# Linear attention beside a gated linear unit on one core: the query features transposed in 32x32 blocks by VectorE and stored feature-major, in place of 128x128 transposes by TensorE in the output stage

## The chip, the cores and the metric

The kernel runs on one core of one Trainium2 chip. The metric is the device time of one execution in microseconds (us). The profiler's engine names are used: PE is TensorE, DVE is VectorE, ACT is ScalarE, POOL is GpSimd, SP is SyncE, which here issues the DMA transfers. All data is float32; matmul operands are written as a rounded high part and a rest (type fp32r), so that three matmuls make one product.

## The reference, cut to what matters

```python
xn = layernorm(x)                                  # x: [2048, 1024]
qkv = xn @ wqkv                                    # 32 heads of 32
pq, pk = q @ w_phi, k @ w_phi                      # per head
phi_q = concat([softmax(pq), softmax(-pq)])        # 64 features a head
phi_k = concat([softmax(pk), softmax(-pk)])
kv, z = phi_k.T @ v, sum(phi_k)                    # per head
s = (phi_q @ kv) / (phi_q @ z + 1e-6) @ wo
h = sigmoid(xn @ w_gate) * (xn @ w_up)             # F = 3584
g = silu(h @ w_down)
out = x + s * g
```

The changed part is phi_q: 2048 tokens with 32 x 64 = 2048 features each. It is made with tokens on partitions, since softmax and the denominator reduce over features; the product phi_q @ kv contracts over features, so it wants features on partitions.

## The kernel before, in words

The large products are done by a seven-product scheme (B11, B21, T2, T3, T4, T1, B22 name its products), each product as three matmuls at lines 145 to 147 (`mm3`). The stages run one after another on TensorE: layer norm and projections, the GLU in passes (in the second of them the k features and kv sums of all heads are made beside it), then the down product and the output stage.

**The down product** has 112 steps: 84 of 24 matmuls, then 28 of 12. For each step SP loads a weight block (line 916) and one or two blocks of h (line 918), ScalarE writes the high part of each (line 136) and VectorE the rest (line 137); both together are a split. `tick()` counts groups of 12 matmuls; `later(n, f)` asks for work n ticks on. In this stage 32 units of query features, 16 token tiles t by two halves hb of the heads, are finished, one every 24/5 ticks (`q_late`). A unit is a buffer `e` of 128 tokens by 1024 features. For t from 6 on it is made here: extremes (663, 664), differences (673, 674), exponentials (ScalarE, 677), sums and reciprocals (682, 683). The 12 units with t under 6 were made earlier, stored in `e_d`, and are loaded again. All are weighed with z on GpSimd (995), reduced to the denominator on VectorE (1000 to 1006), scaled on GpSimd (1013) and stored to `e_d` by one transfer of 512 KB (1016). A scheduler that simulates the engines at build time sets the order on each engine here, within what `behind()` ties to the matmuls.

**The output stage** runs over eight pairs of token tiles. In a pair, (hb, q) names a quarter of the features, 512 of them. `e_load` (1042) brings 128 tokens u by a quarter, `transposes` (1052) turns it with four TensorE transposes into a PSUM bank, and `phi_part` writes from that bank the high part (ScalarE, 1064) and the rest (VectorE, 1066), 512 columns each; the two tiles u of the pair lie side by side. `numerators` (1076) multiplies with kv (`nm` in the table below, four matmuls each), `numerators_out` copies one half of the bank (ScalarE, 1083, `cp`) and adds the other (VectorE, 1085, `ad`). `o_sum` (GpSimd, 1090) and `o_part` (1099, 1101) make the operands of the output product of the next pair; `products` (`g`, groups of three matmuls), `product_out` (`v`), `scaled` (GpSimd, 1957 and 1958, `m` and `a`) and `store` finish the current one. The first pair's features are turned by `attend()` beside the last 14 steps of the down product. For the other seven the written-out table `PAIR` fixes the order on all five engines: `tr`, `hi`, `lo`, `e` are the steps just named, with the digits of u, hb and q; a trailing + or - shifts a name to the next or the previous pair. The last pair's products follow a table `LAST`.

Of the kernel before, what the change touches and what calls it, by code (L numbers as in the profile page):

```python
# [18 lines left out]
P = 128  # L19
# [8 lines left out]
HB = 512  # L28
EPS_LN = 1e-5
# [20 lines left out]
def hedgehog_glu_kernel(  # L50
# [28 lines left out]
    e_d = dram.tile([TT, 2, P, 2 * HB], F32, name="e_d")  # L79
# [35 lines left out]
    QA = 6  # L115
# [550 lines left out]

    def spread(st, p, e):
# [124 lines left out]
    def z_broadcast(hb, i):  # L792
# [4 lines left out]
        nc.scalar.copy(zacc[:, i * HB:(i + 1) * HB], kvb[i])  # L797
        if i:
            nc.sync.dma_start(zb_d[hb], zacc)
# [141 lines left out]
    eqr = Ring((50, 51, 24, 25))  # L941
# [5 lines left out]
    def q_steps(at, t, hb):  # L947
# [16 lines left out]
        for n, f in ((0, load), (5, first), (6, lambda: spread(hold[2], *hold[:2])), (8, lambda: exponentials(hold[1])),  # L964
                     (9, sums), (10, keep)):
            later(at + n, f)

    def q_late(at, t, hb):
# [16 lines left out]
        def second():  # L985
            hold["e"] = whole(eqr.next())
            spread(hold["st"], hold["p"], hold["e"])
# [9 lines left out]
        def density():  # L997
# [4 lines left out]
            den = st[:, 4]  # L1002
            nc.vector.tensor_reduce(den, d2.rearrange("p (h t) -> p h t", t=2), axis=AX.X, op=ALU.add)
            nc.vector.tensor_scalar_add(den, den, EPS_DEN)
            nc.vector.reciprocal(den, den)
            nc.vector.tensor_mul(r2.rearrange("p (h t) -> p h t", t=2), r.rearrange("p (h t) -> p h t", t=2),
                                 den[:, :, None].to_broadcast([P, 16, 2]))
# [6 lines left out]

        def keep():
            nc.sync.dma_start(e_d[t, hb], hold["e"])
# [3 lines left out]
        for n, f in steps + ((11, weigh), (14, density), (15, scale), (18, keep)):  # L1020
            later(at + n, f)
# [10 lines left out]
    tpr, nmr, amm = Ring(banks[:2]), Ring(banks[2:4]), Ring(banks[4:])  # L1032
# [6 lines left out]
    def e_load(u, q):  # L1039
        tp_, hb = divmod(e_next[u, q], 2)  # L1040
        if tp_ < NTP:
            nc.sync.dma_start(slots[47 + u][:, q], e_d[2 * tp_ + u, hb, :, q * HB:(q + 1) * HB])
        e_next[u, q] += 1

    tbank, nbank, half = {}, {}, set()

    def transposes(u, hb, q):
        tbank[u, hb, q] = ps = tpr.next()
        e = whole(47 + u)
        for j in range(4):  # L1050
            k = 4 * q + j
            nc.tensor.transpose(ps[:, j * P:(j + 1) * P], e[:, k * P:(k + 1) * P], ident)  # L1052
        if (hb, q) in half:
            half.remove((hb, q))
        else:
            half.add((hb, q))
            b = run(phu.next(), 2).rearrange("p a b n -> p (a b n)")
            units_ph[hb, q] = b.rearrange("p (a k t) -> p a k t", a=2, t=256)

    def phi_part(part, u, hb, q):  # L1060
        ph, cs = units_ph[hb, q], slice(u * P, (u + 1) * P)
# [993 lines left out]
```

## Time and profile before

| what | value |
|---|---|
| median of three runs | 2331.45 us (2328.89 to 2331.76) |
| span of the profiled execution | 2328.9 us |
| the profiled execution's own time | 2328.89 us, the lowest of the three |
| granted TensorE clock | 0.999 |
| down product | 1577 to 2117 us of the span |
| first transposes of the output stage, last | 2075 us, 2294 us |
| query units stored | 1630 to 2035 us |

Times in the trace count from the span's start. A row of a group reads: line, engine, operation, output<-inputs, shapes, count, then busy us and mean ns of one, then the engine's idle time just before and what ended it. The matmuls are pipelined: one of 512 columns is shown as 0.39 us long, and the next starts 0.23 us after it, so distances between starts are read and not lengths. VectorE's rows overlap in the same way by 0.08 us.

### The profile page before, as it was taken

Reading aid. Unit: us, or ns where it says so; the run is one execution under the profiler, and the core shown is the slowest. Engines: PE = TensorE matmul, PEld = TensorE weight load, DVE = VectorE, ACT = ScalarE, POOL = GpSimd, SP = SyncE. Lnnn points to the kernel's source line nnn. Section 1 sums busy time; section 2 is a strip of 40 time slices with the busy share of each in tenths; the row PEclk is TensorE's granted clock in tenths of the full one; section 3 lists DMA queues with packets and bytes.
Section 4 is the critical chain, followed back from the end, with each engine's and each line's share of the span. In section 5 each row is a group of like instructions: output and inputs, shape, how many; then the busy total and the mean of one; then the engine's idle time right before and its main releaser. Section 6 shows DMA issues by size and latency. Waiting matters only on the chain.

```text
span 2328.9 us, 32696 instructions
## 1 busy us (share of the span) xinstructions
PE 2319.8 (100%) x10789; PEld 1935.0 (83%) x10789; DVE 1712.7 (74%) x2139; ACT 1235.9 (53%) x1997; POOL 1132.2 (49%) x813
## 2 busy tenths in 40 slices
PE   9999999999999999999999999999999999999999
PEld 8888888888888888888888888888888888888887
DVE  8615777886888865688884655666999888977776
ACT  7345577776555555554555555553454345355553
POOL 1324436782141045656654576674665435424556
PEclk9999999999999999999999999999999999999999
DMA  8799977988878777887896866779777666885665
GB/s 300 253 321 355 348 295 270 351 330 285 286 268 287 263 274 249 307 307 270 280 318 210 313 223 220 246 251 369 265 264 266 213 213 203 284 295 207 209 209 167
DMA packets 307322, 631.36 MB, mean 271 GB/s; under 512 B 37840, under 2 KB 38096, under 8 KB 302544
## 3 DMA queue, kind: packets, MB, share of 16 engines
q1 hardware_dynamic: 307152, 629.28, 78.1%
q8 instruction: 84, 1.38, 0.2%
q14 instruction: 86, 0.70, 0.1%
HBM read 378.34 MB, written 250.81 MB: 270 GB/s over the span
## 4 chain that ended last, share of the span: by engine, by line
PE 94%; DMA 2%; DVE 2%; POOL 1%; issue 1%; ACT 1%; SPq 0%; ACTq 0%; POOLq 0%; DVEq 0%
PE bank L145 30%; PE bank L146 29%; PE bank L147 29%; PE bank L380 1%; PE bank L1076 1%; PE bank L1052 1%; PE bank L735 1%; DMA x<-w_phi 1%; DMA x<-x 0%; DMA wd_d<-fa 0%; DMA fc<-e_d 0%; DVE p L729 0%; DMA fc<-qkv_d 0%; DVE w L137 0%; DVE fc L719 0%
## 5 line engine op out<-in xcount | busy, mean ns | idle before, releaser
L145 PE MATMUL bank<-x,w 128*128 128x512 f32 x2248 | 874.6, 390 | 1.3 <-ACT bank L1392 1.2
L146 PE MATMUL bank<-x,w 128*128 128x512 f32 x2248 | 875.1, 389 | 0.0
L147 PE MATMUL bank<-x,w 128*128 128x512 f32 x2248 | 874.5, 389 | 0.0
L137 DVE TENSOR_TENSOR w<-fa,w 128x512 fp32r<-128x512 f32 (+2 forms) x394 | 392.7, 1002 | 270.3 <-ACT w L136 260.3
L145 PEld LDWEIGHTS bank<-x,w 128*128 128x128 f32 x2248 | 422.2, 188 | 89.3 <-ACT bank L1392 2.1
L147 PEld LDWEIGHTS bank<-x,w 128*128 128x128 f32 x2248 | 422.1, 188 | 87.6
L146 PEld LDWEIGHTS bank<-x,w 128*128 128x128 f32 x2248 | 422.2, 188 | 86.2
L136 ACT CAST w<-fa 128x512 fp32r<-128x512 f32 (+2 forms) x394 | 268.2, 684 | 338.1 <-PE bank L146 209.7
L145 PE MATMUL bank<-w,x 128*128 128x512 f32 x708 | 277.6, 392 | 0.0
L147 PE MATMUL bank<-w,x 128*128 128x512 f32 x708 | 276.1, 390 | 0.2 <-DVE x L1251 0.2
L146 PE MATMUL bank<-w,x 128*128 128x512 f32 x708 | 275.7, 389 | 0.0
L147 PEld LDWEIGHTS bank<-w,x 128*128 128x128 f32 x708 | 132.9, 188 | 28.8 <-DVE x L1251 1.4
L145 PEld LDWEIGHTS bank<-w,x 128*128 128x128 f32 x708 | 133.0, 188 | 26.3
L146 PEld LDWEIGHTS bank<-w,x 128*128 128x128 f32 x708 | 133.0, 188 | 26.1
L137 DVE TENSOR_TENSOR w<-fb,w 128x512 fp32r<-128x512 f32 (+1 forms) x116 | 111.7, 964 | 50.4 <-ACT w L136 49.9
L136 ACT CAST w<-fb 128x512 fp32r<-128x512 f32 (+1 forms) x116 | 70.3, 607 | 108.7 <-PE bank L146 80.6
L137 DVE TENSOR_TENSOR x<-fb,x 128x512 fp32r<-128x512 f32 (+1 forms) x87 | 89.9, 1036 | 21.6 <-ACT x L136 21.2
L137 DVE TENSOR_TENSOR p<-fc,p 128x512 fp32r<-128x512 f32 (+1 forms) x68 | 56.4, 839 | 44.6 <-ACT p L136 42.7
L1396 ACT COPY fc<-bank 128x512 f32<-128x512 f32 x116 | 66.5, 583 | 39.5 <-PE bank L147 18.0
L1090 POOL TENSOR_TENSOR fc<-fc 128x512 f32<-128x512 f32 x32 | 48.8, 1526 | 62.5 <-DVE fb L1101 20.9
L136 ACT CAST x<-fb 128x512 fp32r<-128x512 f32 (+1 forms) x87 | 65.3, 753 | 12.4 <-DMA fb<-xr_d 5.1
L677 ACT ACTIVATE fc<-fc 128x1024 f32<-128x1024 f32 x44 | 46.6, 1060 | 33.1 <-DVE fc L674 32.9
(412 smaller groups left out, 3817.1 us busy)
## 6 DMA issues: line engine op xcount, KB each, us to landing
m_d<-fc SPq DMA_DIRECT2D x168, 256.0 KB, 4.3
fa<-h_d SPq DMA_DIRECT2D x152, 256.0 KB, 4.3
fa<-wf_d SPq DMA_DIRECT2D x32, 1024.0 KB, 7.2
x<-m_d SPq DMA_DIRECT2D x128, 256.0 KB, 4.9
fa<-w_gu SPq DMA_DIRECT2D x102, 256.0 KB, 5.1
h_d<-fc SPq DMA_DIRECT2D x102, 256.0 KB, 5.1
fc<-qkv_d SPq DMA_DIRECT2D x86, 256.0 KB, 5.0
fb<-w_gu SPq DMA_DIRECT2D x72, 256.0 KB, 5.1
```

The source lines that it names most:

```text
L136: nc.scalar.copy(o[0], src)
L137: i = nc.vector.tensor_sub(o[1], src, o[0].bitcast(F32))
L145: nc.tensor.matmul(o, a[0], b[0], start=first, stop=False, **kw)
L146: nc.tensor.matmul(o, a[0], b[1], start=False, stop=False, **kw)
L147: last_mm[:] = [nc.tensor.matmul(o, a[1], b[0], start=False, stop=last, **kw).ins]
L380: nc.tensor.matmul(ps[:, gs], r[:, gs], bd[:, 4 * f + g], start=g == 0, stop=g == 3, skip_group_check=True)
L677: nc.scalar.activation(e, e, AF.Exp)
L735: nc.tensor.matmul(kvb[g // 2][:, g % 2 * 256:g % 2 * 256 + 256], v[:, g].rearrange("p a f -> p (a f)"), ph[:, g].rearrange("p a f -> p (a ...
L1052: nc.tensor.transpose(ps[:, j * P:(j + 1) * P], e[:, k * P:(k + 1) * P], ident)
L1076: nc.tensor.matmul(ps[:, j * 256:(j + 1) * 256], kg[:, k], ph[:, a, k], start=a == 0, stop=a == 1)
L1090: nc.gpsimd.tensor_sub(o, a, b)
L1396: nc.scalar.copy(o, banks[b])
```

## The change

1. In `q_late`, VectorE transposes each unit in 32x32 blocks (`turn`, one instruction of 128x1024) and four stores of 128 KB, instead of one of 512 KB, write it to `et_d` with features on partitions. `e_d` keeps only the units with t under 6.
2. So that blocks of 32 give whole features, the order of the features within `e` changes: `spread_q` writes them as (b t k d), and z (`z_broadcast`) and the scale factors follow it. The sum and the addition of the small constant (1003, 1004) become one instruction.
3. In the output stage the TensorE transposes go. `e_load` reads both tiles u for a quarter q straight into one buffer, and `phi_part` works from that buffer in SBUF, 1024 columns at a time.
4. The four PSUM banks for transposes and numerators all serve numerators. The table `PAIR` is written anew without `tr` and with one `hi` and `lo` a quarter.
5. Smaller moves: z is kept in `e_k` instead of `zacc`, one `x_nest_load` comes three ticks later with another buffer, and block x5 stays plain float32 until the last 14 steps, since it holds the transposed units.

```diff
+    def spread_q(st, p, e):
+        pv, mx, mn = [a.rearrange("p (k b d) -> p k b d", b=2, d=d) for a, d in ((p, DH), (st[:, 0], 1), (st[:, 1], 1))]
+        mx, mn = [a.to_broadcast([P, 8, 2, DH]) for a in (mx, mn)]
+        ev = e.rearrange("p (b t k d) -> p t k b d", b=2, t=2, d=DH)
+        nc.vector.tensor_tensor(ev[:, 0], pv, mx, op=ALU.subtract)
+        nc.vector.tensor_tensor(ev[:, 1], mn, pv, op=ALU.subtract)
...
-        nc.scalar.copy(zacc[:, i * HB:(i + 1) * HB], kvb[i])
+        z = e_k.rearrange("p (c k d) -> p k c d", c=4, d=DH)[:, 4 * i:4 * i + 4]
+        nc.scalar.copy(z, kvb[i].rearrange("p (k c d) -> p k c d", c=4, d=DH))
...
-            nc.vector.tensor_reduce(den, d2.rearrange("p (h t) -> p h t", t=2), axis=AX.X, op=ALU.add)
-            nc.vector.tensor_scalar_add(den, den, EPS_DEN)
+            nc.vector.scalar_tensor_tensor(den, d2[:, :, 0], EPS_DEN, d2[:, :, 1], op0=ALU.add, op1=ALU.add)
...
+        def turn():
+            hold["et"] = whole(etr.next())
+            nc.vector.transpose(hold["et"], hold["e"])
+
         def keep():
-            nc.sync.dma_start(e_d[t, hb], hold["e"])
+            for c in range(4):
+                nc.sync.dma_start(et_d[t, hb, c * DH:(c + 1) * DH].rearrange("f (a x) -> a f x", a=4),
+                                  hold["et"][:, c * 256:(c + 1) * 256])
...
-        for n, f in steps + ((11, weigh), (14, density), (15, scale), (18, keep)):
+        for n, f in steps + ((11, weigh), (14, density), (15, scale), (18, turn), (18, keep)):
...
-            nc.sync.dma_start(slots[47 + u][:, q], e_d[2 * tp_ + u, hb, :, q * HB:(q + 1) * HB])
+            nc.sync.dma_start(slots[47 + q][:, u].rearrange("p (a x) -> p a x", a=4),
+                              et_d[2 * tp_ + u, hb].rearrange("p (a q x) -> p q a x", a=4, q=2)[:, q])
...
-        for j in range(4):
-            k = 4 * q + j
-            nc.tensor.transpose(ps[:, j * P:(j + 1) * P], e[:, k * P:(k + 1) * P], ident)
...
+        hi, lo = [units_ph[hb, q][:, a].rearrange("p k (c t) -> p k c t", t=32) for a in range(2)]
+        src = whole(47 + q).rearrange("p (c k t) -> p k c t", k=4, t=32)
         if part == "hi":
-            nc.scalar.copy(ph[:, 0, :, cs], src)
+            nc.scalar.copy(hi, src)
         else:
-            nc.vector.tensor_sub(ph[:, 1, :, cs], src, ph[:, 0, :, cs].bitcast(F32))
+            nc.vector.tensor_sub(lo, src, hi.bitcast(F32))
...
     PAIR = """
-        tr100 gB110 mT4- xT4h- gB111 vB22- xT4l- gB112 mT1- gB113 hi100 lo100 e110 tr001 gT20 hi001 aT1- lo001 e011 gT21 tr000
+        gB110 mT4- xT4h- gB111 vB22- xT4l- gB112 mT1- hi00 gB113 gT20 lo00 aT1- e10 gT21 hi01 aT4- vB11 gT22 lo01 e11 gT23
...
```

Three places show what the change does to the order of instructions. Line numbers of the changed kernel lie a little higher: 137 is 138 there, 1006 is 1016, and the high part and rest of phi, 1064 and 1066, are 1070 and 1072.

First, VectorE in the down product, in the units near the end. Tiles `w` and `x_2` are split parts of the step operands, `sa` and `stq` the small statistics of a unit, `fc` and `x_6` its features, `x_3` the transposed unit. Before:

```order
L1003 TENSOR_REDUCE sa_14546<-sa_14546 128x16
L1004 TENSOR_SCALAR sa_14546<-sa_14546 128x16
L1005 RECIPROCAL sa_14546<-sa_14546 128x16
L1006 TENSOR_TENSOR sa_14546<-stq_14373,sa_14546 128x32
L137 TENSOR_TENSOR w_94<-fa_97,w_94 128x512
L663 TENSOR_REDUCE stq_14576<-fb_99 128x16
L664 TENSOR_REDUCE stq_14576<-fb_99 128x16
L137 TENSOR_TENSOR x_2_5912<-fa_97,x_2_5912 128x512
L673 TENSOR_TENSOR fc_100<-fb_99,stq_14576 128x16x32
L674 TENSOR_TENSOR fc_100<-stq_14576,fb_99 128x16x32
L137 TENSOR_TENSOR w_94<-fa_97,w_94 128x512 x2
```

The same place in the changed kernel:

```order
L1014 SCALAR_TENSOR_TENSOR sa_14612<-sa_14612 128x16
L1015 RECIPROCAL sa_14612<-sa_14612 128x16
L1016 TENSOR_TENSOR sa_14612<-stq_14432,sa_14612 128x32
L138 TENSOR_TENSOR w_95<-fa_98,w_95 128x512
L664 TENSOR_REDUCE stq_14641<-fb_100 128x16
L665 TENSOR_REDUCE stq_14641<-fb_100 128x16
L138 TENSOR_TENSOR x_2_5913<-fa_98,x_2_5913 128x512
L673 TENSOR_TENSOR fc_101<-fb_100,stq_14641 128x8x2x32
L674 TENSOR_TENSOR fc_101<-stq_14641,fb_100 128x8x2x32
L138 TENSOR_TENSOR w_95<-fa_98,w_95 128x512 x2
L1026 STREAM_TRANSPOSE x_3_9793<-x_6_12000 128x1024
```

Two short instructions became one, and the transpose stands eight instructions behind line 1016 here; over the 32 units between 1 and 12 instructions lie between the two.

Second, SP in the down product, around the store of a unit (`wd_d` and `h_d` are the operands of the steps). Before:

```order
L916 DMA fa_97<-wd_d 128x512
L918 DMA fa_97<-h_d 128x512 x2
L1016 DMA e_d<-x_6_12000 128x1024
L918 DMA fa_97<-h_d 128x512
L918 DMA fb_0_98<-h_d 128x512
L916 DMA fb_0_98<-wd_d 128x512
```

The changed kernel near there:

```order
L928 DMA fa_98<-h_d 128x512 x2
L1030 DMA et_d<-x_3_9793 4x32x256 x3
L926 DMA fa_98<-wd_d 128x512
L1030 DMA et_d<-x_3_9793 4x32x256
L990 DMA fb_100<-qkv_d 128x512
L928 DMA fa_98<-h_d 128x512
```

Four stores stand where one stood, with loads of the steps between and behind them.

Third, ScalarE early in a pair of the output stage (`fb` and `x_4` are the two operand buffers of phi, banks hold transposes or numerators, 1936 and 1940 take the first product out). Before:

```order
L1936 COPY fb_0_98<-bank_105 128x512
L1064 CAST x_4_11997<-bank_102 128x4x128
L1083 COPY fc_100<-bank_103 64x2x2x128
L1083 COPY fc_100<-bank_104 64x2x2x128
L1083 COPY fc_100<-bank_103 64x2x2x128
L1064 CAST fb_15845<-bank_101 128x4x128
L1064 CAST fb_15845<-bank_102 128x4x128
L1083 COPY fc_100<-bank_104 64x2x2x128
```

In the changed kernel:

```order
L1940 COPY fb_0_99<-bank_106 128x512
L1089 COPY fc_101<-bank_102 64x2x2x128
L1089 COPY fc_101<-bank_103 64x2x2x128
L1089 COPY fc_101<-bank_104 64x2x2x128
L1070 CAST fb_15942<-fc_101 128x1024
L1089 COPY fc_101<-bank_105 64x2x2x128
L1070 CAST x_4_15940<-fc_101 128x1024
```

The cast of the third quarter (`hi10`) still stands behind the third numerator copy, and covers both token tiles; its input is a buffer in SBUF instead of a bank.

74 lines of the change are left out of this document (32 added, 42 removed).

## The prediction

> **What bounds the kernel now.** I read the page's busy times and its chain first, then the waits of TensorE.
>
> ```profile
> PE 2319.8 (100%) x10789; PEld 1935.0 (83%) x10789; DVE 1712.7 (74%) x2139; ACT 1235.9 (53%) x1997; POOL 1132.2 (49%) x813
> PE 94%; DMA 2%; DVE 2%; POOL 1%; issue 1%; ACT 1%; SPq 0%; ACTq 0%; POOLq 0%; DVEq 0%
> ```
>
> The waits of TensorE (us in all, times, longest):
>
> ```profile
> PE bank L1326 <- POOL ident masks.py:199: 1.5, 1, 1.5
> PE bank L145 <- ACT bank L1392: 1.2, 1, 1.2
> PE bank L1052 <- DMA fc<-e_d: 1.1, 1, 1.1
> PE bank L380 <- POOL fb L1313: 0.3, 1, 0.3
> PE bank L147 <- DVE x L1251: 0.2, 1, 0.2
> ```
>
> These five waits are all that TensorE has, 4.3 us in the whole span. So TensorE is the bound everywhere, and work taken from it is worth its full issue time until another engine makes it wait. The stages that the change touches tell how near the others are. The columns are the stretch, its length, then busy us of PE, PEld, DVE, ACT and POOL, the granted clock, DMA share and GB/s.
>
> ```profile
> 1620.00:2040.00 420.00, 420.00 (x1855) 347.89 (x1854) 381.53 (x551) 187.81 (x309) 220.72 (x157) 1.00 0.73 248
> 1740.00:1800.00 60.00, 60.00 (x267) 49.69 (x266) 58.64 (x84) 26.36 (x44) 35.88 (x27) 1.00 0.83 281
> 1980.00:2020.00 40.00, 40.00 (x178) 33.12 (x177) 39.55 (x57) 12.05 (x21) 21.20 (x15) 1.00 0.93 324
> 2180.00:2260.00 80.00, 80.00 (x447) 68.32 (x446) 63.44 (x88) 41.67 (x72) 47.89 (x33) 1.00 0.60 198
> 880.00:1260.00 380.00, 378.71 (x1742) 315.10 (x1742) 270.86 (x280) 202.05 (x325) 213.05 (x139) 1.00 0.82 284
> ```
>
> In the down product VectorE is idle for only 38.5 of 420 us, and in two stretches for 1.4 of 60 and 0.45 of 40. The change adds VectorE work there. The output stage (three pairs in 80 us, 26.67 us each) leaves VectorE 16.6 us of 80.
>
> **What is removed.** The group of transposes at line 1052, and TensorE's starts around it:
>
> ```profile
> L1052 PE MATMUL bank<-ident,fc x256: 270/272/328, 2075.5 to 2294.0; 128*128 128x128 f32 x128
> ```
>
> ```profile
> 2150.63 0.60 PE L1052 MATMUL bank<-ident,fc 128*128 128x128 f32 x4
> 2151.76 0.60 PE L1052 MATMUL bank<-ident,fc 128*128 128x128 f32 x4
> 2166.05 0.40 PE L145 MATMUL bank<-w,fb 128*128 128x512 f32 x1
> 2166.74 0.39 PE L145 MATMUL bank<-x,x 128*128 128x512 f32 x1
> ```
>
> From the first group of four to the next, with three ordinary matmuls between, is 1.13 us; three ordinary matmuls alone take 0.69. Four transposes therefore cost 0.44 us (their row says 272 ns each, but they overlap). 256 of them, in 64 groups: 64 x 0.44 = **28.2 us off TensorE**, 24.6 of it in the seven pairs (3.52 each), 3.5 in the first pair's part beside the down product. PEld goes with it.
>
> **What is added in the down product.** The trace has no VectorE transpose. The nearest row, 1000, reads 1024 elements of one SBUF buffer in 1.21 us; the bounds I take are twice that, 2.42 (two passes), and half, 0.6.
>
> ```profile
> L1000 DVE TENSOR_REDUCE sa<-fc x32: 1204/1210/1214, 1621.7 to 2024.2; 128x32 f32<-128x1024 f32 x32
> L1003 DVE TENSOR_REDUCE sa<-sa 128x16 f32<-128x32 f32 x32 | 5.5, 171 | 0.1
> L1004 DVE TENSOR_SCALAR sa<-sa 128x16 f32<-128x16 f32 x32 | 12.5, 390 | 0.9
> L1013 POOL TENSOR_TENSOR fc<-fc,sa 128x512 f32<-128x512 f32 x32 | 40.7, 1292 | 19.8 <-DVE sa L1006 19.7
> 2009.63 0.32 SPq L1016 DMA_DIRECT2D e_d<-fc  x1
> ```
>
> I take 1.21 us, the row with the same amount read and one input: 32 x 1.21 = 38.7 us. The joined instruction replaces 18.0 us (1003, 1004) by what I take as 1004's 12.5, so 33.2 us net fill the 38.5 idle ones: VectorE goes to 414.7 of 420. It still fits on the mean; the two full stretches do not. A unit comes every 13.06 us (24/5 ticks of 2.72 us, twelve matmuls), so 1740 to 1800 gets 4.6 x 1.04 = 4.8 us against 1.4 idle, and 1980 to 2020 3.1 against 0.45. What absorbs this is the lead of the splits. Counted back from the last of the 308, the last splits of steps 33 and 80 and their first matmuls are these:
>
> ```profile
> 1752.34 0.68 DVE L137 TENSOR_TENSOR x<-fa,x 128x512 fp32r<-128x512 f32 x1
> 1756.39 0.39 PE L145 MATMUL bank<-x,w 128*128 128x512 f32 x1
> 2007.15 3.00 DVE L137 TENSOR_TENSOR w<-fa,w 128x512 fp32r<-128x512 f32 x2
> 2012.07 0.39 PE L145 MATMUL bank<-x,w 128*128 128x512 f32 x1
> ```
>
> They end at 1753.02 and 2010.15, 3.4 and 1.9 us before they are needed, the least leads in these two stretches. In 1980 to 2020 the lack is 3.1 - 0.45 - 1.9 = 0.8 us, in 1740 to 1800 4.8 - 1.4 - 3.4 = 0. Queued behind a transpose are the splits, and behind those TensorE. The transpose itself can wait for the two scalings on GpSimd (2 x 1.29 = 2.6 us after line 1006), where only one instruction lies between; some two or three such waits of 1 to 2 us fall among the 32. I put the stage's **loss at 2 us**, ends 0 and 8 (all of the lack of 4.8 - 1.4 and 3.1 - 0.45, plus one such wait, with no lead).
>
> On SP three more stores of 0.32 us a unit are 0.96 us in 13.06, and the store waits longer, with loads of the steps behind it. These loads have room; the only waits of splits for h in the run are four early ones, of 14.5 us together, and the landing times say the same of stores and of the reads that shrink to pieces of 512 bytes:
>
> ```profile
> ACT w L136 <- DMA fa<-h_d: 14.5, 4, 6.9
> e_d<-fc SPq DMA_DIRECT2D x16, 512.0 KB, 4.4
> L1042 SPq DMA_DIRECT2D fc<-e_d x64: 319/320/687, 1961.8 to 2285.3; - x64
> DMA to landing us min/median/max: 2.5/3.7/8.8
> ```
>
> Cost 0; without that room, what SP adds, about 1 us at a unit. The moved z, the changed view in `spread_q` (same elements) and the later `x_nest_load` are 0: VectorE is idle for 109 of 380 us where z is made, and 16 us lie between that load and its sums.
>
> **What is added in a pair of the output stage.** One pair's rows, and the kinds:
>
> ```profile
> 2199.13 0.48 PE L145 MATMUL bank<-x,fa 128*128 128x512 f32 x1
> 2209.09 0.64 PE L1076 MATMUL bank<-x,p 128*128 128x256 f32 x4
> 2209.76 0.58 ACT L1083 COPY fc<-bank 64x512 f32<-64x512 f32 x1 [1.09 <-PE bank L1076]
> 2210.36 0.59 ACT L1064 CAST fb<-bank 128x512 fp32r<-128x512 f32 x1
> 2213.41 0.64 PE L1076 MATMUL bank<-fb,p 128*128 128x256 f32 x4
> L136 ACT CAST x<-fb 128x1024 fp32r<-128x1024 f32 x28 | 29.3, 1049 | 8.5 <-DMA fb<-xr_d 5.1 <-DMA fb<-xo_d 3.4
> L719 DVE TENSOR_TENSOR fc<-fc,stk x32: 1208/1218/2314, 601.1 to 1218.9; 128x1024 f32<-128x1024 f32 x32
> L1066 DVE TENSOR_TENSOR x<-bank,x x32: 677/691/693, 2080.9 to 2295.8; 128x512 fp32r<-128x512 f32 x32
> L1101 DVE TENSOR_TENSOR fa<-fc,fa x17: 675/1178/1774, 2135.6 to 2299.7; 128x512 fp32r<-128x512 f32 x17
> L1957 POOL TENSOR_TENSOR fb<-fb,fc x7: 1288/1302/1739, 2174.3 to 2319.7; 128x512 f32<-128x512 f32 x7
> ```
>
> A high part of 1024 columns costs ScalarE 1.05 us (136, same shape) for two of 0.59: neutral. A rest of 1024 costs VectorE 1.22 (719's median) for two of 0.69: neutral too. What is new is a chain. The pair starts at 2199.13; third numerators (`nm011`) start 9.96 us on, fifth (`nm101`) 14.28. Without the transposes before them (3 and 6 groups, 1.32 and 2.64 us) that is 8.64 and 11.64. `cp011` follows `nm011` by 0.67, the next ScalarE row 0.60 later, so `hi10` runs from 9.91 to 10.96 and `lo10` to 12.18. `nm101` wants the rest with its second matmul, at about 11.76: **0.42 us of waiting a pair**, even with nothing in the way; the numerators are now the late ones. `hi11` and `lo11` likewise end near 14.6, half a microsecond before `nm111` at 15.08.
>
> Where the rest read a PSUM bank (1066) it never took over 0.693 us; line 1101, with both inputs in SBUF, takes up to 1.1 us more, about a GpSimd instruction (1957). Line 1072 has both in SBUF. [...]
>
> In the middle I take 0.6 us a pair, since GpSimd's next multiplication waits for a load about then: 7 x 0.6 = **4.2 us**. Ends: 0.42 x 7 = 2.9, and 2.5 x 7 = 17.6 (both `lo10` and `lo11` blocked for 1.29, less the half microsecond).
>
> **The sum.** 2328.9 - 28.2 + 2 + 4.2 = 2306.9 against the profiled execution's own 2328.89. The median of the runs is 2.6 us above that, so 2309.5; I predict **2309 us**. Its own range: 2303 (all waits hidden) to 2317.
>
> **The rivals.**
> - *All of it hides*: the lead in the down product holds and ScalarE reaches `hi10` sooner than the row order says. 2331.45 - 28.2 = 2303. For it: TensorE has waited for nothing there. Against: the 0.42 us follow from a fixed order.
> - *GpSimd locks out the rests in each pair*: 17.6 us in the seven pairs and 2 in the down product leave 2331.45 - 28.2 + 19.6 = 2323. For it: GpSimd is busy 47.89 of 80 us and more densely so in shorter pairs. Against: its operations wait for a load in this part of a pair.
> - *The reads are late*: `e_load` for `hi10` can only go when `lo00` is done, and if four times the pieces take 4.0 us more to land, TensorE waits as much once a pair: 7 x 4.0 = 28, nothing gained, 2331. For it: the maximum of 8.8 us. Against: the median of 3.7, and DMA at a share of 0.60.
> - *VectorE becomes the bound in the down product*: a transpose of two passes, 2.42 us. 32 x 2.42 - 5.5 = 71.9 us of work meet 38.5 idle ones and some 2 us of lead: 31.4 us late, plus 4.2 in the pairs, 2331.45 - 28.2 + 35.6 = 2339, slower. It decides from (38.5 + 2 + 5.5 + 28.2 - 4.2) / 32 = 2.19 us a transpose on. For it: nothing in the trace excludes it. Against: every one-input row of 1024 elements takes 1.2. [...]
> - *The change does not do what it says*: TensorE transposes left. The order shows none on lines 1070 to 1082; not counted.
>
> **How the numbers follow.** Chances: the forecast 0.52, all hidden 0.19, GpSimd 0.13, late reads 0.07, VectorE bound 0.09. A range of 2301 to 2327 holds the first three (0.84) with the spread of the runs and leaves out the last two. A difference of 0.2%, 4.7 us, is about what this kernel's runs can tell from none. Faster by more: the first three, 0.84; the same: late reads, 0.07; slower: 0.09.
>
> **What would show it.** No 128x128 row in the output stage; STREAM_TRANSPOSE near 1.21 us x32; PE's waits list gaining line 1082 <- DVE 1072 at 0.4 to 0.8 us in seven pairs, and a few us of lines 146 to 148 <- DVE 138 near 1755 and 2010; pairs of 23.8 us; DVE over 410 us in the down product's 420. It is wrong if the transpose is far from 1.21 us, if the pairs are under 23.3 or over 25 us, or if TensorE waits mostly for DMA.

## The result, and the profile after

The changed kernel takes 2351.2 us (median of four runs, 2348.3 to 2352.6) against 2330.2 us of the kernel before: a ratio of 1.0087, with a 95% interval of 1.0073 to 1.0102. It is slower by 21 us, where 22 us less was forecast and the range ended at 2327. The profiled execution spans 2346.5 us. In it the busy times, and the chain that ended last, read:

```profile
PE 2307.9 (98%) x10533; PEld 1918.4 (82%) x10533; DVE 1750.8 (75%) x2107; ACT 1231.1 (52%) x1965; POOL 1153.2 (49%) x813
PE 85%; DVE 6%; DMA 5%; issue 2%; SPq 1%; ACT 1%; POOL 1%; DVEq 0%; ACTq 0%; POOLq 0%
```

TensorE has 256 instructions less, and its share of the chain fell from 94% to 85%. The lines of this kernel are 1 higher than before in the helpers (146 to 148 are the three products) and 4 to 15 higher in the stages named here. The waits of TensorE (us in all, times, longest):

```profile
PE bank L1082 <- DVE x L1072: 10.6, 6, 2.4
PE bank L146 <- ACT bank L1811: 7.5, 1, 7.5
PE bank L147 <- DVE x L138: 4.9, 3, 2.5
PE bank L146 <- DMA x<-wo_d: 3.6, 4, 1.3
PE bank L1082 <- DVE fb L1072: 2.8, 7, 0.8
PE bank L146 <- ACT x L137: 2.4, 1, 2.4
PE bank L1331 <- POOL ident masks.py:199: 1.5, 1, 1.5
PE bank L744 <- DVE p L738: 0.5, 1, 0.5
```

Before, five waits made 4.3 us; now they make 33.8, and all but the last two lie behind the start of the down product. The stretches of the prediction, with the same columns (length; busy PE, PEld, DVE, ACT, POOL; clock; DMA share; GB/s):

```profile
1620.00:2040.00 420.00, 412.53 (x1812) 341.07 (x1811) 391.56 (x534) 180.83 (x298) 215.32 (x152) 0.94 0.72 239
1980.00:2020.00 40.00, 40.00 (x179) 33.10 (x178) 38.89 (x50) 14.38 (x23) 24.28 (x17) 0.95 0.82 268
2180.00:2260.00 80.00, 71.90 (x339) 59.48 (x338) 69.70 (x73) 38.89 (x58) 54.88 (x33) 0.91 0.60 191
```

In the output stage TensorE now stands still for 8.1 of 80 us. VectorE, which the forecast saw at 414.7 of 420 us in the down product, reached 391.6 only, and TensorE waited all the same: being full was not what failed. (This execution reads a clock of 0.95 even where nothing changed and as many matmuls start as before, 891 from 200 to 400 us in both; so 0.95 is read as full here, and only the falls below it are used.)

For the experiments I cut each trace into two stretches, by the starts of TensorE's three-part products: the down product from its first step to the first product of the output stage, and from there seven pairs of 84 such matmuls. Each number is one profiled execution; the medians are of the timed runs.

| kernel | median us | down product | seven pairs |
|---|---|---|---|
| before | 2330 | 541.1 | 187.1 |
| changed | 2351.2 | 557.2 | 188.9 |
| e1 vB21 behind lo11 | 2347.2 | 559.2 | 186.5 |
| e2 rest from PSUM | 2341.8 | 556.8 | 181.9 |
| e3 transposes two ticks later | 2347.0 | 554.6 | 192.8 |
| e4 last transposes elsewhere | 2357.2 | 562.4 | 193.9 |
| e5 no block transposes | 2333.3 | 540.8 | 190.4 |
| e6 first high part held | 2343.4 | 548.7 | 191.2 |
| e7 three repairs | 2328.1 | 542.6 | 182.0 |
| e8 no scaling on GpSimd | 2335.0 | 558.7 | 174.9 |
| e9 before, no TensorE transposes | 2306.7 | 537.9 | 166.3 |
| e10 long reads | 2352.2 | 561.4 | 186.7 |
| e11 e7 and vB11 first | 2326.7 | 542.0 | 182.3 |
| e12 e11, PSUM in one half only | 2332.1 | 545.8 | 184.5 |

Where no instruction on the engines was changed in the pairs (changed, e3 to e6, and e10, which changes the pieces of their loads) they took 186.7 to 193.9 us, so a difference of a few us there is not a finding.

**Three places of loss.** The first is at 1729 us of the down product, in time order (start, duration, in brackets the idle time before and what ended it):

```profile
1716.16 2.05 POOL L1022 TENSOR_TENSOR x<-x,sa 128x512 f32<-128x512 f32 x2
1718.24 1.25 DVE L1026 STREAM_TRANSPOSE x<-x 128x1024 f32<-128x1024 f32 x1 [3.21 <-POOL x L1022]
...
1734.91 1.28 DVE L1810 COPY fc<-bank 128x512 f32<-128x512 f32 x2
1735.63 1.19 ACT L1811 COPY bank<-x 128x512 f32<-128x512 f32 x2 [3.92 <-DVE fc L1810]
1736.27 0.79 PE L146 MATMUL bank<-x,w 128*128 128x512 f32 x1 [7.47 <-ACT bank L1811]
1736.86 0.63 PE L147 MATMUL bank<-x,w 128*128 128x512 f32 x1
```

The kernel before, in the same place:

```profile
1727.05 1.28 DVE L1806 COPY fc<-bank 128x512 f32<-128x512 f32 x2
...
1727.77 1.19 ACT L1807 COPY bank<-x 128x512 f32<-128x512 f32 x2 [0.65 <-DVE fc L1806]
```

A block of the down product has ended; VectorE empties its bank, ScalarE fills the bank with the next block's start, and TensorE goes on. VectorE comes to that copy at 1734.91 instead of 1727.05, because it works off a backlog. Since the first unit eight transposes (9.9 us) have stood before this copy, and in front of three of them VectorE waited for GpSimd's scaling, 8.4 us in all; the last of these waits is the 3.2 us above. Line 1026 in the whole kernel, its two shapes of names and what its engine waited for before it:

```profile
L1026 DVE STREAM_TRANSPOSE x<-fc x16: 1183/1232/1246, 1634.2 to 2023.3; 128x1024 f32<-128x1024 f32 x16
L1026 DVE STREAM_TRANSPOSE x<-x x16: 1228/1234/1246, 1658.9 to 2048.4; 128x1024 f32<-128x1024 f32 x16
...
  POOL x L1022: 9.1, 5
  POOL fc L1022: 5.2, 2
```

A transpose takes 1.23 us (1.21 was taken), but VectorE stands in front of seven of them for 14.3 us.

The second place is at 2052 us: ScalarE arrives at the first high part of the attention and stands there.

```profile
2052.70 1.85 SPq L1030 DMA_DIRECT2D et_d<-x  x3
...
2062.05 1.04 ACT L1070 CAST x<-fc 128x1024 fp32r<-128x1024 f32 x1 [9.45 <-DMA fb<-w_down]
```

The brackets name a load, the event that came last by the page. By the trace's semaphore events the last event that this instruction waits for is another, the landing of the last store at 2061.99 us, issued at 2054.04: the stores read buffers of the tile that the high part writes. The casts for the down product are queued behind it, and TensorE waits 2.4 and 2.5 us (lines 146 and 147 of the waits) and then runs slowly. The window from 2068 to 2071.5 us, columns as above:

```profile
2068.00:2071.50 3.50, 3.50 (x9) 2.76 (x10) 3.50 (x3) 1.34 (x3) 2.52 (x2) 0.50 0.78 230
```

Nine matmuls in 3.5 us, at a granted clock of 0.50; a matmul of 512 columns starts every 0.43 us instead of every 0.227.

The third place is every pair. One of them, in time order:

```profile
2243.83 1.74 POOL L1961 TENSOR_TENSOR fb<-fb,fc 128x512 f32<-128x512 f32 x1
2244.34 2.31 DVE L1072 TENSOR_TENSOR fb<-fc,fb 128x1024 fp32r<-128x1024 f32 x1
2245.65 2.15 POOL L1962 TENSOR_TENSOR fb<-fb,fc 128x512 f32<-128x512 f32 x1
2246.58 2.31 DVE L1072 TENSOR_TENSOR x<-fc,x 128x1024 fp32r<-128x1024 f32 x1
2247.77 2.27 POOL L1962 TENSOR_TENSOR p<-p,fc 128x512 f32<-128x512 f32 x1
...
2251.30 0.43 SPq L1902 DMA_DIRECT2D fc<-g_d  x1
...
2256.92 0.69 DVE L1946 TENSOR_TENSOR fc<-fc,bank 128x512 f32<-128x512 f32 x1 [2.15 <-DMA fc<-g_d]
2257.53 1.87 DVE L1072 TENSOR_TENSOR x<-fc,x 128x1024 fp32r<-128x1024 f32 x1
2259.46 0.95 PE L1082 MATMUL bank<-x,p 128*128 128x256 f32 x3 [2.05 <-DVE x L1072]
```

The rests (1072) and GpSimd's scalings (1961, 1962) take turns: the two rests take 1.09 us more than the 1.22 of others, the two scalings of line 1962 0.86 and 0.98 us more than 1.29, and each of these four ends 1.08 to 1.15 us, about its short length, after the other engine's instruction that was running when it started. This is called the lock in what follows. The groups (minimum, median, maximum in ns), of the changed kernel:

```profile
L1072 DVE TENSOR_TENSOR x<-fc,x x16: 1205/1898/2317, 2063.1 to 2312.6; 128x1024 fp32r<-128x1024 f32 x16
L1962 POOL TENSOR_TENSOR p<-p,fc x7: 1296/2269/2277, 2176.4 to 2334.5; 128x512 f32<-128x512 f32 x7
```

and GpSimd's same instruction in the kernel before:

```profile
L1958 POOL TENSOR_TENSOR p<-p,fc x7: 1283/1287/1295, 2160.7 to 2315.7; 128x512 f32<-128x512 f32 x7
```

The late scalings free the buffers of g late, the late rests free those of the next features, and both loads go through SP in order. So g lands late, `vB21` (1946) waits for it on VectorE, and the rest `lo11` behind `vB21` is 2 us late for TensorE. `lo11` itself also takes turns, with the scaling by the g that has just landed: 1.87 us here instead of 1.22, and 1.86 to 1.93 in four of the seven pairs.

A fourth, smaller place is the first pair: the wait for x<-wo_d in the list above, 3.6 us in four waits from 2155.9 to 2161.1 us. It is in every run with the change (2.2 to 4.5 us) and in none without; no experiment was aimed at it.

### The profile page after: what moved, and what is told of

The parts are those of the page before. It is cut to its first block, busy times and chain, and to the rows that moved or that the text cites. A ratio compares the mean times of both kernels' runs of the same rounds, so it can differ in the third digit from the quotient of the medians.

```text
span 2346.5 us, 32121 instructions
## 1 busy us (share of the span) xinstructions
PE 2307.9 (98%) x10533; PEld 1918.4 (82%) x10533; DVE 1750.8 (75%) x2107; ACT 1231.1 (52%) x1965; POOL 1153.2 (49%) x813
## 4 chain that ended last, share of the span: by engine, by line
PE 85%; DVE 6%; DMA 5%; issue 2%; SPq 1%; ACT 1%; POOL 1%; DVEq 0%; ACTq 0%; POOLq 0%
PE bank L147 27%; PE bank L148 27%; PE bank L146 27%; DMA fc<-g_d 2%; PE bank L381 1%; PE bank L744 1%; DMA fa<-h_d 1%; DVE x L1072 1%; DVE x L1107 1%; DVE fb L1072 1%; DMA et_d<-x 1%; DVE w L138 1%; DMA fa<-w_down 0%; DVE x L138 0%; DMA fc<-et_d 0%
## 5 line engine op out<-in xcount | busy, mean ns | idle before, releaser
L686 ACT ACTIVATE fc<-fc 128x1024 f32<-128x1024 f32 x44 | 46.6, 1060 | 45.2 <-DVE fc L683 27.5
```

Of the source, the lines that this page charges most:

```text
L686: nc.scalar.activation(e, e, AF.Exp)
```

## The experiments

**e9: what the removal is worth.** In the kernel before, `transposes` keeps its buffers and issues nothing.

```
-        for j in range(4):
-            k = 4 * q + j
-            nc.tensor.transpose(ps[:, j * P:(j + 1) * P], e[:, k * P:(k + 1) * P], ident)
```

> The kernel before, with nothing changed but that TensorE's 256 transposes are left out: the high parts and rests are made from what stands in the two banks, so the numerators are computed from other data, in the same instructions. This is what the removal is worth on TensorE where nothing else is added. If a group of four costs 0.44 us, as read from the starts (forecast): 28.2 us less, about 2301 to 2302 us, no new wait over 0.3 us in the pairs. If the groups partly hid in gaps between other matmuls (the sums of the matmuls' usual spacings in the changed kernel are only 22 us shorter than before): 2306 to 2309 us.

Measured: 2306.7 us, ratio 0.9904 (0.9891 to 0.9918) to 2329.0. That is 22.3 us, 0.35 a group of four and not 0.44. A pair takes 23.75 us instead of 26.58: 2.83 less, where 8 x 0.44 = 3.52 were forecast. Counting the starts inside one pair, the numerators now follow each other at 0.148 us instead of 0.121 (25 of them, 0.7 us): while the transposes were there, part of their cost lay under the transposes. Why, was not tried. This kernel is the floor for the rest: from it, the changed kernel loses 557.2 - 537.9 = 19.3 us in the down product and 188.9 - 166.3 = 22.6 in the pairs. -22.3 + 19.3 + 22.6 = 19.6 of the 21 us measured.

**e5: the transposes' share of the down product.**

```
-            hold["et"] = whole(etr.next())
-            nc.vector.transpose(hold["et"], hold["e"])
+            hold["et"] = hold["e"]
```

> VectorE's 32 block transposes are left out: the four stores of a unit take the weighted features as they stand, so that the output stage computes with features that are not put feature-major. All else is the changed kernel (2351.2 us). Theory V (the transposes' 38.7 us on VectorE, with the waits in front of them, are what the down product loses): TensorE's stall of 7.5 us for the bank at 1729 us and the half clock behind it go, and so does the wait of the first high part, since slots 20 to 23 are then not written by late transposes; the down product loses under 2 us instead of 19.5: about 2332 us. Theory H (the stall comes from the longer stores, whose landing of 8 us holds buffers): the stall of 7.5 us stays at over 4 us, 2343 us or more.

Measured: 2333.3 us, as theory V had it (2332). The down product falls to 540.8 us: 16.4 of its 19.3 us of loss are the transposes' doing. That is the first and the second place together, since the buffers that the high part waited for are no longer written. Of the 2.9 us left, 2.7 are two waits for a rest at the end of the stage (line 147). The same window as above:

```profile
1620.00:2040.00 420.00, 419.89 (x1853) 347.48 (x1852) 378.51 (x516) 187.08 (x308) 223.58 (x157) 1.00 0.73 244
```

VectorE is busy 13 us less there than in the changed kernel, not 38.7, partly because TensorE no longer stalls and more of the program falls into the window (1853 matmuls instead of 1812); and its busy time holds waiting for GpSimd too, as shown further down. The pairs keep their loss (190.4).

**e3: is VectorE full, or does it stand?**

```
-        for n, f in steps + ((11, weigh), (14, density), (15, scale), (18, turn), (18, keep)):
+        for n, f in steps + ((11, weigh), (14, density), (15, scale), (20, turn), (20, keep)):
```

> The block transposes and their stores come two ticks (5.4 us) later: tick 20 of a unit instead of 18. Theory W (VectorE stands in each transpose waiting for GpSimd's scaling, 14.3 us in seven waits, and its lead is spent on that): these waits go to under 3 us, the stall of 7.5 us of TensorE at 1729 us for the bank that ScalarE fills behind VectorE's copy goes, and the half clock behind it: about 2341 us. Theory F (VectorE is simply full with 33 us more work): the waits move elsewhere, the stall stays at 4 us or more; 2347 to 2352 us.

Measured: 2347.0 us. Its waits of TensorE:

```profile
PE bank L146 <- ACT x L137: 6.0, 1, 6.0
...
PE bank L146 <- ACT bank L1811: 1.3, 1, 1.3
```

VectorE waits for GpSimd in front of no transpose, and the stall of 7.5 us is 1.3: theory W holds, with all 32 transposes still on VectorE. VectorE comes to the copy of the first place at 1729.01 us, 2.0 us after the kernel before, with seven transposes ahead of it: the rest of the 7.9 us was mostly the waits. The time did not fall to 2341. The last stores are issued 1.5 us later (the last at 2055.55 instead of 2054.04) and TensorE, which has not stalled, comes to that place earlier, so the first high part now makes it wait 6.0 and 2.3 us instead of 2.4 and 2.5; the pairs came out 3.9 us longer too, within what they vary by.

**e4 and e6: what the first high part waits for.** In e4 the last two units' transposes go to buffers that are not in the tile that the high part writes:

```
-    eqr, etr = Ring((50, 51, 24, 25)), Ring((20, 21, 22, 23))
+    eqr, etr = Ring((50, 51, 24, 25)), Ring((20, 21, 22, 23) * 7 + (20, 21, 50, 51))
```

> The last two units' transposes write slots 50 and 51 instead of 22 and 23, so that the first high part of the attention, which writes slot 20 of the same tile, need not wait for the landing of their stores. Theory S (stores): ScalarE's wait of 9.4 us at 2052 us, in front of the casts for the down product, goes, TensorE's two waits of 2.4 and 2.5 us at 2064 and 2067 go, and the half clock of 3.4 us behind them: about 2344 us. Theory D (the page names the load fb<-w_down as what ended the wait: late loads): the wait stays, for w_down; 2349 to 2352 us.

Measured: 2357.2 us, worse, which neither theory had.

```profile
2025.07 4.24 SPq L1030 DMA_DIRECT2D et_d<-x  x4
...
2036.77 1.04 ACT L1070 CAST x<-fc 128x1024 fp32r<-128x1024 f32 x1 [17.13 <-DMA fa<-w_down]
```

The order is made from modelled times. With the tile free two units earlier, the high part stands further ahead on ScalarE, and waits there until 2036.77 us for the stores of the unit before those two, which read slot 21 and were issued from 2025.07 to 2029.31; TensorE waits 8.3 us in one piece behind it. So e4 did not test the theory, and e6 does it without touching a store: the attention's instructions are put behind the last ones issued at that place.

```
+    def held_back(f, *a):
+        with behind():
+            f(*a)
...
-            side.extend([lambda fn=fn, a=a: fn(*a) for fn, *a in attend()])
+            side.extend([lambda fn=fn, a=a: held_back(fn, *a) for fn, *a in attend()])
```

> The instructions of the attention are put behind the last ones issued on ScalarE, VectorE and SP at that place, so that the first high part stands on ScalarE 24 casts later than in the changed kernel, at about the step that it belongs to, and the stores have landed by then. Theory S (it waited for the last stores' landing and held the casts behind it): TensorE's waits of 2.4 and 2.5 us at 2064 and 2067 us go with the 3.4 us of half clock behind them: 2343 to 2345 us. Theory D (the casts wait for late loads of w_down in any case): these waits stay within 2 us of their sum, 2348 us or more.

Measured: 2343.4 us, down product 548.7 instead of 557.2. Its waits of TensorE on lines 146 and 147:

```profile
PE bank L146 <- ACT bank L1811: 7.9, 1, 7.9
...
PE bank L147 <- DVE x L138: 1.1, 1, 1.1
```

The waits at 2064 and 2067 us are gone and the one at 1729 stays: theory S. The page names the load of w_down as what ended ScalarE's wait, but that is only what landed last before it; the same loads are there in e6.

**e1: is it the order on VectorE?** It tries theory Q against theory L, which e8 and e2 try further: GpSimd's instructions hold the rests, wherever these stand. By theory L `lo11` is held again here, and the time is 2347 to 2351 us.

```
-        nm010 lo10 e00+ w0 w1 aB22- gT30 w2 w3 cp010 ad010 hi11 vB21 gT31 nm101 lT1- yB22- cp101 lo11 e01+ gT32 aB21 ad101
+        nm010 lo10 e00+ w0 w1 aB22- gT30 w2 w3 cp010 ad010 hi11 gT31 nm101 lT1- yB22- cp101 lo11 vB21 e01+ gT32 aB21 ad101
```

> One token moves in the pair's order: vB21 (VectorE's multiplication by g, line 1946) goes behind lo11. Everything else is the changed kernel, whose median is 2351.2 us. Theory Q (the rest lo11 is late because it stands on VectorE behind vB21, which waits 2.2 to 2.4 us for its load of g): the waits of TensorE for lo11 (10.6 us in six waits at line 1082) go, and with them the half clock behind them (19 matmuls, 3.8 us); about 2337 us, pairs of about 25.3 us instead of 27.3. [...]

Measured: 2347.2 us, pairs 186.5. Two of its waits:

```profile
PE bank L146 <- DVE fc L1944: 5.5, 3, 2.2
...
PE bank L1082 <- DVE x L1072: 1.3, 1, 1.3
```

The wait for lo11 fell from 10.6 us to 1.3 and came back as a wait for the bank that line 1944 empties, behind the moved `vB21`. So the link that theory Q names is there (`lo11` was late behind `vB21`), but its time is not reached, and the pairs came down by no more than they vary by. Theory L's time came, though not by its reason: `lo11` takes 1.21 to 1.23 us in the last four pairs and is no longer held. As long as g is late, something on VectorE is late; why g is late, this run does not show.

**e8: GpSimd's scalings left out.** They are issued no more in the seven pairs: three blocks of a pair go without the multiplication by g and the addition of x, and the fourth without the addition; loads and stores stay.

```
-        if part == "m":
-            return last or eng.tensor_mul(y, y, g)
+        if eng is nc.gpsimd or part == "m":
+            return eng is nc.gpsimd or last or eng.tensor_mul(y, y, g)
```

> GpSimd's scalings (multiplication by g, then addition of x; 1.29 us each alone, four to seven a pair) are left out of the seven pairs, so three of the four blocks of a pair are stored without them; the loads of g and x stay. Theory L (lock): the rests of a pair's start take 1.22 instead of 2.31 us, the loads of the next e go 2 us earlier, and only the 0.5 us a pair for lo10 stay of 18.4 us of waits: about 2336 us, pairs of 24 to 24.5. Theory Q (queue of loads): vB21 on VectorE still waits about 2 us for g and lo11 behind it: pairs of over 26 us, 2345 us or more.

Measured: 2335.0 us (2336 expected by theory L). The rests, and the stretch of the pairs:

```profile
L1072 DVE TENSOR_TENSOR x<-fc,x x16: 1208/1211/1225, 2063.6 to 2299.6; 128x1024 fp32r<-128x1024 f32 x16
```

```profile
2180.00:2260.00 80.00, 77.96 (x384) 64.87 (x384) 67.35 (x85) 43.78 (x66) 22.80 (x15) 1.00 0.69 223
```

No rest takes over 1.23 us, and 14.0 of the pairs' 22.6 us of loss are gone. Of the 8.6 left, 5.4 lie in the first pair (29.3 us against e9's 23.9), where TensorE waits 3.6 us for loads of wo_d, and the other six lose 0.3 to 0.8 each. This experiment removes the scalings' claims on g as well, so by itself it does not tell the lock from the load of g; the next one does. And `vB21` still waits for g here, 6.1 us in five waits from 2180 to 2300 us against 8.9 in four in the changed kernel, so the lock is not the only thing that makes g late; but `lo11`, not held any more, costs TensorE only 2.4 us.

**e2: the scalings kept, the lock removed.** ScalarE writes the high part a second time into two PSUM banks, and VectorE subtracts that one, so that it has one input in SBUF.

```
-    nmr, amm = Ring(banks[:4]), Ring(banks[4:])
+    nmr, amm = Ring(banks[2:4]), Ring(banks[4:])
...
-    nbank = {}
+    nbank, hp = {}, [b.bitcast(F32R).rearrange("p (k c t) -> p k c t", k=2, t=32) for b in banks[:2]]
...
-        if part == "hi":
-            nc.scalar.copy(hi, src)
-        else:
-            nc.vector.tensor_sub(lo, src, hi.bitcast(F32))
-
+        for j in range(2):
+            if part == "hi":
+                nc.scalar.copy(hp[j], src[:, 2 * j:2 * j + 2])
+            else:
+                nc.vector.tensor_sub(lo[:, 2 * j:2 * j + 2], src[:, 2 * j:2 * j + 2], hp[j].bitcast(F32))
+        part == "hi" and nc.scalar.copy(hi, src)
```

> ScalarE writes the high part a second time, into two PSUM banks, and VectorE takes the rest from there (two instructions of 512 columns, one input in PSUM instead of both in SBUF); the numerators' banks go back from four to two. Theory L (lock): the rests of the start of a pair take 2 x 0.69 instead of 2.31 us, GpSimd's scalings 1.29 instead of 2.15 to 2.27, the loads of g and of the next e go out 2 us earlier, and no wait over 1 us is left in the pairs: about 2337 us. Theory Q (queue): the rests get shorter, but vB21 still waits for g for about 2 us and lo11 behind it: pairs of over 26.5 us, 2346 us or more.

Measured: 2341.8 us, ratio to before 1.0051 (1.0036 to 1.0066), halfway between the two theories' times; the rows decide. GpSimd's scaling, and the longest sum of waits in the pairs:

```profile
L1962 POOL TENSOR_TENSOR p<-p,fc x7: 1267/1293/1299, 2177.0 to 2325.4; 128x512 f32<-128x512 f32 x7
```

```profile
PE bank L1082 <- DVE fc L1091: 3.4, 7, 0.5
```

The scaling is back at 1.29 us, as before the change, and no wait in the steady pairs is over 0.7 us: 25.4 us a pair, though all the scalings and loads of g are there, and from 2180 to 2300 us `vB21` waits for g nowhere. Theory L holds. It stops 1.7 us short of e9's 23.75. The second copy costs ScalarE 2 x 0.58 us for each unit and the numerators have two banks instead of four; what each of these is worth was not separated.

**e10: the length of the pieces.** et_d is laid out for reads of 2 KB, and the stores write pieces of 512 bytes.

```
-                nc.sync.dma_start(et_d[t, hb, c * DH:(c + 1) * DH].rearrange("f (a x) -> a f x", a=4),
-                                  hold["et"][:, c * 256:(c + 1) * 256])
+                nc.sync.dma_start(et_d[t, hb, c * DH:(c + 1) * DH].rearrange("f (q a x) -> a f q x", a=4, q=2),
+                                  hold["et"][:, c * 256:(c + 1) * 256].rearrange("p (q x) -> p q x", q=2))
...
-            nc.sync.dma_start(slots[47 + q][:, u].rearrange("p (a x) -> p a x", a=4),
-                              et_d[2 * tp_ + u, hb].rearrange("p (a q x) -> p q a x", a=4, q=2)[:, q])
+            nc.sync.dma_start(slots[47 + q][:, u],
+                              et_d[2 * tp_ + u, hb, :, q * HB:(q + 1) * HB])
```

> In the changed kernel, et_d is laid out so that the output stage reads pieces of 2 KB instead of 512 bytes, and the stores beside the down product write pieces of 512 bytes instead of 1 KB. Rival of the late reads (the short pieces make the loads of the features and of g behind them late): the pairs' 18.4 us of waits fall by 8 us or more, 2343 us or less. If the lock and not the pieces makes them late: 2349 to 2353 us, and rather at the upper end, since the shorter pieces of the stores land later and the first high part waits for them.

Measured: 2352.2 us, pairs 186.7. The short reads are not what makes the loads late.

**e7, e11, e12: can it be repaired?** e7 joins e2, e3 and e6.

> The rest from PSUM (second experiment), the transposes two ticks later (third) and the attention's instructions held back, together. If the three losses are separate (theory of three causes): 2351.2 - 9.4 as in the second experiment, - 9 for the stall at 1729 us and its half clock, - 7.5 for the first high part: about 2325 us, 5 us below the kernel before. If they stand for one another (VectorE has too much work in both stages, and a wait that is taken away comes back elsewhere): 2333 us or more.

Measured: 2328.1 us, ratio 0.9993 (0.9984 to 1.0003): 23 us better than the changed kernel, the same as the kernel before. Alone the three repairs are worth 9.4, 4.2 and 7.8 us, 21.4 together. That speaks for separate losses, though the expectation's 2325 was missed by 3 us: the down product is at 542.6 us, 4.7 above the floor. No granted clock below 1.00 is left before the end of the span, and the largest sum of waits is the numerators' two banks:

```profile
PE bank L1082 <- DVE fc L1091: 4.9, 9, 0.8
```

e11 puts `vB11` before `hi01` in the pair's order.

> The three repairs of the seventh experiment, and in the pair's order vB11 (ScalarE's copy of the first block, line 1940) ahead of hi01. In the seventh, TensorE waits 0.5 to 0.6 us a pair for that copy, which stands behind 2.2 us of ScalarE's second unit. If that wait goes and none comes in its place: 7 x 0.6 = 4 us less than 2328.1, about 2324 us. If the second unit's rest, now 0.6 us later, makes TensorE wait for lo01 instead: 2328 us or more.

Measured: 2326.7 us, ratio 0.9991 (0.9982 to 1.0000). The wait for 1940 went, and that for 1091 grew from 4.9 to 9.2 us: most of it came back. e12 takes the rest from PSUM in the first half of a pair only.

```
+    nmr, amm = (Ring(banks[2:4]), Ring(banks[:4])), Ring(banks[4:])
...
+        for j in range(0 if hb else 2):
...
+        elif hb:
...
-        nbank[hb, q, b] = ps = nmr.next()
+        nbank[hb, q, b] = ps = nmr[hb].next()
```

> As the eleventh kernel, but the rest comes from PSUM only in the first half of a pair (hb 0), where GpSimd is at its scalings; in the second half, where GpSimd waits for its load of g, the rest has both inputs in SBUF again and the numerators have four banks instead of two. If the waits left in the eleventh (9.2 us at the numerators for VectorE's line 1091, their bank's emptying) come from the two banks: 5 to 7 us less than 2326.7, about 2320 to 2322 us, pairs of 24.4 us. If the rests of the second half are held by GpSimd again (lock) or stand behind vB21 (queue): 2326 us or more.

Measured: 2332.1 us, ratio 1.0005 (0.9996 to 1.0014). With three lines more, 1077 is the rest with both inputs in SBUF and 1949 is `vB21`:

```profile
PE bank L1085 <- DVE x L1077: 8.8, 6, 2.0
```

```profile
DVE p L1949 <- DMA fc<-g_d: 8.2, 3, 4.0
```

```profile
L1077 DVE TENSOR_TENSOR x<-fc,x x8: 1209/1510/1907, 2097.6 to 2295.8; 128x1024 fp32r<-128x1024 f32 x8
```

The banks' waits went and the old chain, g to `vB21` to `lo11`, came back, though the scalings at the start of a pair no longer meet a rest with both inputs in SBUF. `lo11` is again held by GpSimd, 1.28 to 1.91 us in the pairs. So the lock at the start of a pair, where the rests of 2.31 us stand, is not the whole loss: the second half with both inputs in SBUF is enough for most of TensorE's waits for `lo11`. Whether they begin with the lock on `lo11` or with the order of the loads on SP stays open. None of the three is faster than the kernel before by more than its measurement tells.

## Why the prediction was wrong, step by step

- **What is removed: 28.2 us, measured 22.3 (e9).** Mis-sized. The 0.44 us were read between two starts, as if the numerators would stay as they were; they take 0.7 us a pair more without the transposes between them.
- **The transpose: 1.21 us, measured 1.23.** Right, and so the fourth rival (two passes) is out, though the sign that it forecast came.
- **The loss in the down product: 2 us, ends 0 and 8; measured 19.3, of which 16.4 by the transposes (e5).** This step failed. It asked whether the splits still come before their matmuls, and they nearly did: of 33.8 us of waits, 7.3 are for a split (4.9 for a rest, 2.4 for a high part), and 4.9 of these stand behind the first high part of the attention. What came late first was VectorE's other duty for TensorE, to empty a bank so that ScalarE can fill it (7.5 us), which has no lead at all. The prediction had put the transposes' waits for GpSimd at "some two or three such waits of 1 to 2 us"; there were seven of 14.3 us together, and e3 shows that they, more than the 38.7 us of work, made the backlog.
- **"VectorE is idle for only 38.5 of 420 us": the sum took busy for work.** The trace of the kernel before shows that part of the busy time is waiting for GpSimd already. One row there:

```profile
L1001 DVE TENSOR_TENSOR sa<-sa,stq x20: 185/1275/1284, 1623.4 to 2015.5; 128x32 f32<-128x32 f32 x20
```

An instruction on 32 columns that can end in 0.19 us takes 1.28 in the median, about one GpSimd instruction (1.29). Of the 32 on this line, under both names of its input, the 24 of 1.27 or 1.28 us all run beside a GpSimd instruction, and five of the six of 0.18 or 0.19 us beside none. Splits that can end in 0.69 us take up to 1.83. What lies above the short times comes to about 90 of the 381.5 busy us (an estimate: 62 from lines 137, 673 and 674, 27.5 from line 1001). So the idle time could not tell how much work the stage still takes.

- **SP's stores: cost 0, "these loads have room".** Right for the loads, wrong as a whole. It did not ask who writes next into the buffers that the stores read: the first high part, on an engine with TensorE's casts behind it. This step failed too: 7.8 us (e6).
- **A pair's new chain, 0.42 us for lo10.** Right: 2.8 us in seven waits, and 0.3 to 0.8 a pair in e8. **"`hi11` and `lo11` likewise end near 14.6, half a microsecond before `nm111`"** failed; this is the step behind the 4.2 us put for the pairs, which measured 22.6. The chain was taken along ScalarE and VectorE's own work; `vB21`, which stands between them and waits for a load, was left out.
- **The rival of GpSimd's lock, 0.13, priced at 17.6 us in the pairs, was the cause of most of it there** (14.0 by e8, which also removes the scalings' use of g; 7.0 by e2, net of what its repair costs), but in part in another place. It was put at `lo10` and `lo11`, and GpSimd was said to wait for a load in that part of a pair. `lo10` was never held. `lo11` was, by 0.65 us in four pairs, by the scalings that start when that load lands. The longest locks, 2.31 instead of 1.22 us, fell on `lo00` and `lo01` at the start, which TensorE does not wait for; as far as their price is paid, it is through the buffers and SP's order half a pair later, and e12 shows that this is not the whole way. The rival of the late reads saw the order on SP but blamed the length of the pieces, which e10 excludes.
- **What was not in the sum at all: a wait costs more than its length.** Of the matmuls of 512 columns, 20 in the down product and 19 in the pairs ran at half clock behind a wait, at 0.43 instead of 0.227 us: 39 x 0.2 = 7.9 us. They are part of the 19.3 and the 22.6.

With the measured terms the sum comes to 2330.2 - 22.3 + 19.3 + 22.6 = 2349.8, against 2351.2. The rest is within the runs' spread. The two losses are differences of stretches of the same traces, so the sum divides the loss and does not test its causes; the experiments do that.

## What to carry to other kernels

Before work is put on an engine with little room, list everything that the bound engine gets from it, bank hand-overs before splits, and look for instructions that would stand there waiting for a third engine: their waiting can fill the queue faster than their work (e3 took away the waits alone, and the stall of 7.5 us became 1.3). Do not read busy time as work: look at the shortest and the median duration of one instruction first (0.19 and 1.28 us on line 1001). When a buffer between two engines moves from PSUM to SBUF, check who else reads SBUF at the time (a rest of 1.22 us took up to 2.31 beside GpSimd's scalings), and follow the delay through the buffers it frees and the queue of loads that waits for them. And a buffer that a store reads is busy until the store has landed (8.0 us after its issue at the second place): see which engine writes it next, and what is queued there.

## What the runs showed of the hardware

- **Half clock behind waits.** In the changed kernel TensorE has seven waits of 2.0 us or more (7.5; 2.4 and 2.5 close together; 2.2, 2.4, 2.1 and 2.0), and behind them six stretches of 3.4 or 6.8 us at a granted clock of 0.50; behind its waits of up to 1.6 us there is none. e7, whose waits in and behind the down product are 1.2 us at most, has none. It is no sharp bound: in e3 two waits of 2.0 and 2.2 us stayed without, and in e8 a stretch of 3.4 us stands behind two of 1.4 and 1.8 us.
- **VectorE's rests and GpSimd's scalings took turns.** With both inputs of VectorE's subtraction in SBUF, 1.22 became 2.31 us and GpSimd's 1.29 became 2.27; with one input in PSUM GpSimd's were back at 1.29 (e2) and VectorE's took 0.68 for each half.
- **A VectorE transpose of 128x1024 f32 in blocks of 32x32 takes 1.23 us**, about as long as a reduction of the same shape (1.21, line 1000 of the kernel before), and none of the 32 took over 1.25 us, the seven that ran beside a GpSimd instruction included.
- **The short stores of a unit landed later than the one long store.** By the trace's semaphore events the 128 stores of 128 KB landed 3.2 to 8.6 us after issue, 6.4 in the median (the last of them 8.0); the 32 of 512 KB in the kernel before 2.6 to 7.3, 4.0 in the median.
